# Mish as one ScalarE activation, the key norms' root on VectorE, and a new instruction order in a fused delta-rule and feed-forward kernel

## The chip, the cores and the metric

The kernel runs on one core of a Trainium2 chip. The core has the engines TensorE (PE; PEld is its weight load), VectorE (DVE), ScalarE (ACT), GpSimd (POOL) and SyncE (SP); each runs its own list of instructions in order, and they wait for each other by semaphores. SP and ACT also start DMA transfers here. Matmuls write to PSUM. The metric is the device time of one execution in microseconds (us), the median of several runs.

## The reference, cut to what matters

```python
def _attn_ref(q, k, v, beta):            # B 4, H 8, S 768, D 48
    k_n = k / (np.linalg.norm(k, axis=-1, keepdims=True) + 1e-06)
    for t in range(S):
        y[:, :, t] = q_t @ state
        state = state + beta_t * outer(k_t, v_t - state.T @ k_t)

def _moe_ref(x, w_in, w_out):            # x 3072x384, d_ff 2048
    h = x @ w_in
    sp = np.where(h > 20.0, h, np.log1p(np.exp(np.minimum(h, 20.0))))
    g = h * np.tanh(sp)
    return (g @ w_out).astype(np.float32)
```

The loop is shortened to its algebra (`k_t` stands for the normalised key). `x` is the first part's `y` with the heads put side by side. The function h · tanh(softplus(h)) is called Mish. `w_in` and `w_out` arrive as 64-bit floats; all else is 32-bit.

## The kernel before

**Delta rule in blocks.** The 768 steps are cut into 12 blocks of 64, and 32 batch-head pairs sit in 16 tile columns (`NP`) of two halves. Inside a block the recurrence is solved as a triangular system in two 32-row parts; across blocks a state is carried. `early(g)` prepares the blocks 2g and 2g+1, for g from 0 to 5: it transposes k (`kt`, line 1721), forms the Gram blocks k·k on PE (`pg`, line 1752), masks them into `d` (line 1755) and transposes `d` to `gt` (line 1763) so that one partition holds a whole 32x32 triangle. The diagonal of `gt` is the squared norm of the keys (`ss`); its root `y` is made on ACT by Ln and Exp (lines 1773 and 1774), and DVE forms the factor `nb` with a reciprocal and a few operations on 32 columns. The triangle is scaled by it (line 1790) and solved column by column with a product (`pr`, line 1806) and an addition (line 1808). For g below `FG` = 2 the triangle is *split*: two 16x16 triangles, 14 steps, and a later `merge(n)` for each of the four blocks. A merge has small matmuls `ma` (line 1860) and `mb` (line 1871), an ACT copy `ym`, a DVE addition into `tt` (line 1874) and a transpose; split solves end with transposes to `tu` (line 1816) and `tt` (line 1818). For g of 2 and more the whole triangle is solved in 30 steps; it ends with transposes to `d` (line 1825) and `tn` (line 1829), and POOL copies `d` to `tt` (`place`, line 1841).

**The stages of a block** on PE, in the helper of line 1936, are named by their tiles: `ta` and `tb` (solved triangles applied to the second Gram part), `gq` (queries), `pz` and `py`. Block 2's `ta` is the first thing that needs early 1. The block's output is transposed and split into a high and a low part of x (ACT line 2063, DVE line 2065), both held in a format that PE multiplies exactly enough in three products.

**Feed-forward in units.** Each block gives 256 rows of x. A unit (n, fp), 12 x 8 of them, takes 256 of the 2048 columns: 18 matmuls of 128x256 into `h` (line 2089; two buffers of PSUM), then a chain of eight steps to `g`, then 12 matmuls of 128x384 into `acc` (line 2126). The chain: Exp from `h` on ACT (2103), clamp and +1 on DVE (2104), Square, Ln and Exp on ACT (2105 to 2107), the product with `h` on DVE (2108), a copy to the high part of `g` on ACT (2109) and the subtraction for the low part on DVE (2110). The weights are held negated, which the signs in the chain take into account.

**Weights.** `convert` turns 28 weight parts (12 of `w_in`, 128x512, and 16 of `w_out`, 128x384) from 64-bit patterns to high and low 32-bit parts: a clamp on DVE (line 1665), a Prelu on ACT that adjusts the exponent with its sign (line 1667), a shift and a combination on DVE (1674, 1676), the high part on ACT (1680) and the low part on PE and ACT or on DVE (1697).

**Order.** The order of the instructions of the five engines is fixed by hand: the table `TN` and a long table of numbers ahead of it give each step of each piece (`early0`, `cv5`, `merge2`, `g1.0.3.0>2` and so on) its place, and pieces also wait for labels given by others. Loads go over SP's queue by the helper of line 1621, some over ACT's; k and the second block's q are loaded 32 and then 16 columns wide, after the unused part of the tile was set to zero (line 1710). The `warm` matmuls (line 2152) multiply zeros and have no use in the result.

Of the kernel before, what the change touches and what calls it, by code (L numbers as in the profile page):

```python
# [28 lines left out]
def bcast_in(ap, n):  # L29
# [10 lines left out]
    'loada': [5],  # L40
    'early0': [6, 7, 8, 9, 10, 13, 20, 22, 23, 24, 25, 26, 28, 29, 30, 31, 32, 33, 34, 37, 38, 39, 40, 41, 42, 44, 45, 46, 53, 54, 55, 56, 57, 58, 59, 60, 61],
    'loadv': [11],
    'early0.2>1': [12],
    'early0.1>1': [14],
    'early0.4>1': [15],
    'loadi1': [16],
    'cv0': [69, 17, 87, 96, 113, 114, 134, 166, 164],
    'loads': [18],
    'early0.5>1': [19],
# [19 lines left out]
    'turn_q(0,1,(1,))': [74],
    'turn_q(0,1,(0,))': [75],  # L70
    'cv4': [76, 107, 132, 155, 219, 228, 230, 231, 189],
    'warm30.6': [77],
    'warm29.5': [78],
    'loadi3': [79],
    'unit(1,)': [80],
    'turn_q(0,0,(1,))': [81],
    'cv5': [82, 121, 199, 200, 201, 202, 203, 233, 212],
    'loadp': [83],
# [2319 lines left out]
```

## Time and profile before

| | us |
|---|---|
| median of 3 runs | 689.33 |
| lowest and highest | 685.59, 690.51 |
| the profiled execution | 684.56 |
| its span in the profile | 682.8 |

PE is busy 635.3 us of the span, DVE 489.9, ACT 430.3, POOL 72.1. The profile's page groups instructions by line, engine and tile. A row such as "L2108 DVE SCALAR_TENSOR_TENSOR e<-e,h" gives the tile written and those read, how often, the busy time, the mean of one in ns, the idle time of the engine ahead of them and what ended most of that. A row of waits names the waiting engine, tile and line, then whom it waited for; "issue" stands for time in which no wait is seen. The weight of a wait depends on whether the engine that waits is the one that sets the end of its stretch.

### The profile page before, as it was taken

To read this page: it belongs to the slowest core of one execution; us is meant where nothing else is said; L and a number is where in the kernel's file an instruction comes from. 1 tells how busy PE (TensorE), PEld (TensorE's weight loads), DVE (VectorE), ACT (ScalarE), POOL (GpSimd) and SP (SyncE) were. 2 spreads that over 40 slices of the span, in tenths; PEclk is the share of its full clock that TensorE was granted. 3 is DMA by queue.
4 is the path that set the end of the run, shared out by engine and by line. 5 is a ranking of instruction groups with operands and counts; after the bars stand their busy time and mean duration, and the time that the engine had idled before them with its cause. 6 is when DMAs were issued, how large, how long until landed. Compare 5 with 4: busy or idle time off the path is not lost.

```text
span 682.8 us, 23514 instructions
## 1 busy us (share of the span) xinstructions
PE 635.3 (93%) x10203; PEld 577.8 (85%) x10203; DVE 489.9 (72%) x1042; ACT 430.3 (63%) x802; POOL 72.1 (11%) x119
## 2 busy tenths in 40 slices
...
GB/s 154 164 285 216 213 1 26 1 48 49 5 48 49 64 19 45 62 22 56 36 33 53 45 35 42 48 37 26 42 42 35 22 42 48 25 20 7 1 24 23
DMA packets 161510, 37.79 MB, mean 55 GB/s; under 512 B 154720, under 2 KB 157792, under 8 KB 161408
## 3 DMA queue, kind: packets, MB, share of 16 engines
...
q10 hardware_dynamic: 6464, 0.69, 0.8%
q14 instruction: 22, 0.18, 0.1%
...
## 4 chain that ended last, share of the span: by engine, by line
PE 43%; DVE 35%; ACT 8%; issue 6%; DMA 4%; SPq 4%; ACTq 0%; DVEq 0%
PE h L2089 15%; PE acc L2126 15%; DVE gt L1808 5%; DVE pr L1806 5%; DVE e L2108 4%; DVE g L2110 3%; SPq L1621 3%; DVE xx L1987 3%; PE gq L1936 3%; DVE xx L1923 2%; DMA kt<-in_k_dram 2%; DVE gt L1763 2%; DVE e L2104 2%; DMA xx<-in_q_dram 2%; PE pg L1752 2%
## 5 line engine op out<-in xcount | busy, mean ns | idle before, releaser
L2089 PE MATMUL h<-x,wi 128*128 128x256 f32 x1728 | 232.1, 289 | 17.3 <-DVE e L2108 5.4
L2089 PEld LDWEIGHTS h<-x,wi 128*128 128x128 f32 x1728 | 218.9, 192 | 25.2 <-DVE e L2108 6.7
L2126 PE MATMUL acc<-wo,g 128*128 128x384 f32 x1152 | 225.5, 344 | 4.4 <-DVE g L2110 2.2
L2126 PEld LDWEIGHTS acc<-wo,g 128*128 128x128 f32 x1152 | 199.8, 190 | 10.8 <-DVE g L2110 6.1
L2108 DVE SCALAR_TENSOR_TENSOR e<-e,h 128x512 f32<-128x512 f32 x96 | 65.7, 684 | 76.8 <-ACT e L2107 75.3
L2105 ACT ACTIVATE e<-e 128x512 f32<-128x512 f32 x96 | 60.6, 631 | 54.1 <-DVE e L2104 53.3
L2109 ACT CAST g<-e 128x512 fp32r<-128x512 f32 x96 | 59.3, 618 | 48.5 <-DVE e L2108 47.0
L2110 DVE TENSOR_TENSOR g<-e,g 128x512 fp32r<-128x512 f32 x96 | 68.4, 713 | 28.8 <-ACT g L2109 27.7
L2103 ACT ACTIVATE e<-h 128x512 f32<-128x512 f32 x96 | 57.2, 595 | 42.7 <-PE h L2089 34.2
L2107 ACT ACTIVATE e<-e 128x512 f32<-128x512 f32 x96 | 60.6, 632 | 2.7
L2106 ACT ACTIVATE e<-e 128x512 f32<-128x512 f32 x96 | 60.6, 631 | 2.5
L2104 DVE TENSOR_SCALAR e<-e 128x512 f32<-128x512 f32 x96 | 41.6, 435 | 26.2 <-ACT e L2103 25.8
L1808 DVE TENSOR_TENSOR gt<-gt,pr 128x84 f32<-128x84 f32 (+14 forms) x148 | 51.3, 346 | 3.5
L1806 DVE TENSOR_TENSOR pr<-gt 128x84 f32<-128x84 f32 (+14 forms) x148 | 49.8, 337 | 3.5
L1936 PE MATMUL gq<-xx,kt 48*64 48x112 f32 (+1 forms) x768 | 44.5, 260 | 2.2 <-DVE xx L1923 1.3
L1936 PE MATMUL py<-xx 128*64 128x48 f32 x768 | 43.5, 227 | 2.9 <-ACT xx L2009 2.9
L1936 PEld LDWEIGHTS py<-xx 128*64 128x64 f32 x768 | 39.5, 141 | 7.8 <-ACT xx L2009 3.8
L1936 PEld LDWEIGHTS gq<-xx,kt 48*64 48x64 f32 x768 | 38.3, 136 | 4.4 <-DVE xx L1923 2.2
L1987 DVE TENSOR_TENSOR xx<-gq,amask 64x256 f32<-64x256 f32 x96 | 40.2, 418 | 0.7
L1936 PE MATMUL ps<-xx 128*48 128x48 f32 x704 | 39.0, 211 | 0.4 <-DVE xx L1987 0.2
L1936 PEld LDWEIGHTS pz<-vt,tt 64*64 64x64 f32 x768 | 32.7, 135 | 5.1 <-issue 2.9
L1936 PE MATMUL pz<-vt,tt 64*64 64x48 f32 x768 | 36.6, 231 | 0.0
...
## 6 DMA issues: line engine op xcount, KB each, us to landing
...
```

Of the source, the lines that this page charges most:

```text
L1806: nc.vector.tensor_tensor(out=pv, in0=nj, in1=xj, op=ALU.mult)
L1808: nc.vector.tensor_tensor(out=below, in0=below, in1=pv, op=ALU.add)
L1936: last[:] = [nc.tensor.matmul(*a, start=True, stop=True)]
L1987: nc.vector.tensor_tensor(out=x[r, p4, hh, D:D + C], in0=ps[r, :, d:], in1=bcast_mid(amask[r], 4), op=ALU.mult)
L2089: nc.tensor.matmul(h[:, f2, :], wt["i", f * P // WI * NCH + c][:, i2, f0:f0 + P], x[:, c, :], start=(i == 0), stop=(i == 3 * NCH - 1))
L2105: (0.65, lambda: nc.scalar.activation(e, e, AF.Square)),
L2106: (0.65, lambda: nc.scalar.activation(e, e, AF.Ln, bias=0.5, scale=0.5)),
L2107: (0.7, lambda: nc.scalar.activation(e, e, AF.Exp, scale=-1.0)),
L2108: (0.8, lambda: nc.vector.scalar_tensor_tensor(e, e, -1.0, h, op0=ALU.add, op1=ALU.mult)),
L2109: (0.7, lambda: nc.scalar.copy(out=gg[:, 0], in_=e)),
L2110: (0.8, lambda: eng.tensor_tensor(out=gg[:, 1], in0=e, in1=gg[:, 0], op=ALU.subtract))):
L2126: nc.tensor.matmul(acc[t], gg[:, a, f2, ts_], wt["o", f][:, i2, :], start=(f == 0 and i == 0), stop=(f == NF - 1 and i == 2))
```

## The change

1. The unit's chain has three steps in place of eight: one ACT activation Mish from `h`, with scale -1 for the negated weights, then the copy and the subtraction as before. The very first Mish (block 0) is ordered behind the Prelu of the first 14 weight parts.
2. Weight parts from the 15th on (`KP` = 14; six of 128x512 and eight of 128x384) use an ACT multiplication and one more DVE operation in place of the Prelu.
3. `FG` is 1: early 1 is solved as a whole triangle with 30 steps, merges 2 and 3 do not exist, and POOL's `place` copies blocks 2 and 3.
4. Unsplit Gram blocks are written by the mask operation in the order in which the transpose then reads them contiguously; the transpose to `tn` reads `d`, contiguous too. For g of 1 and more the root of the norms is made on DVE: an integer first guess and two Newton steps, eleven operations on 32 columns in place of ACT's Ln and Exp. For g = 0 Ln and Exp stay.
5. The second half of k (and of block 1's q) is loaded 32 wide, reading into the next row, and the memsets go, but for the last block.
6. The table of places is a new one. ACT has five table loads in place of one; the last stands before the first Mish.

```diff
-    TN = dict(tl=4.0, fg=2, pl=[*range(0, 8)], po=8, ...
+    TN = dict(tl=4.0, fg=1, pl=[*range(0, 8)], po=8, ...
...
-    'merge2': [564, 565, 571, 577],
...
+    def wide_rows(src, hh):
+        flat = src.rearrange("hh t (b h) d -> (hh b h t d)", b=2)
+        rows = flat[32:B * H * S * D - (D - 32)].rearrange("(m d) -> m d", d=D)
+        m0 = hh * (NP * S - C)
+        return rows[m0:m0 + NP * S, 0:32].rearrange("(p t) d -> t p d", t=S)
...
-        nc.scalar.activation(hf, hf, AF.Prelu, scale=2.0 ** -112, alpha=-2.0 ** 32)
+        if k < KP:
+            nc.scalar.activation(hf, hf, AF.Prelu, scale=2.0 ** -112, alpha=-2.0 ** 32)
+            give(f"s{k}")
+        else:
+            nc.scalar.mul(out=hf, in_=hf, mul=2.0 ** -112)
+            yield
+            nc.vector.scalar_tensor_tensor(hf, hf, -2.0 ** 32, hf, op0=ALU.mult, op1=ALU.max)
...
-        for r in (slice(32, 64), slice(96, 128)):
-            (nc.vector if n < 2 else nc.gpsimd).memset(kts[n][r, :, :, D - 32:], 0.0)
...
+                    to = dt[:, t2, pr, :] if split else dg[:, t2, pr, :]
...
+            nc.vector.transpose(gr.rearrange("p a b -> p (a b)")[:, :32 * 32], dt.rearrange("p a b f -> p (a b f)"))
...
-        nc.scalar.activation(y, ss, AF.Ln, scale=0.25)
-        nc.scalar.activation(y, y, AF.Exp, scale=0.5)
+        if g:
+            nc.vector.tensor_scalar(ss, ss, 0.25, None, op0=ALU.mult)
+            yi = y.bitcast(I32)
+            nc.vector.tensor_scalar(yi, ss.bitcast(I32), 1, None, op0=ALU.logical_shift_right)
+            nc.vector.tensor_scalar(yi, yi, 0x1FBD1DF5, None, op0=ALU.add)
+            rn = ap.tile([P, 32], F32, tag="rc", name=f"rn{g}", bufs=1)
+            for _ in range(2):
+                nc.vector.reciprocal(rn, y)
+                nc.vector.scalar_tensor_tensor(rn, ss, 1.0, rn, op0=ALU.mult, op1=ALU.mult)
+                nc.vector.tensor_scalar(y, y, 0.5, None, op0=ALU.mult)
+                nc.vector.scalar_tensor_tensor(y, rn, 0.5, y, op0=ALU.mult, op1=ALU.add)
+        else:
+            nc.scalar.activation(y, ss, AF.Ln, scale=0.25)
+            nc.scalar.activation(y, y, AF.Exp, scale=0.5)
...
-            for d, f in ((0.7, lambda: nc.scalar.activation(e, h, AF.Exp, scale=-1.0)),
-                         (0.55, lambda: nc.vector.tensor_scalar(e, e, EXP20, 1.0, op0=ALU.min, op1=ALU.add)),
-                         (0.65, lambda: nc.scalar.activation(e, e, AF.Square)),
-                         (0.65, lambda: nc.scalar.activation(e, e, AF.Ln, bias=0.5, scale=0.5)),
-                         (0.7, lambda: nc.scalar.activation(e, e, AF.Exp, scale=-1.0)),
-                         (0.8, lambda: nc.vector.scalar_tensor_tensor(e, e, -1.0, h, op0=ALU.add, op1=ALU.mult)),
+            for d, f in ((0.7, lambda: nc.scalar.activation(e, h, AF.Mish, scale=-1.0)),
                          (0.7, lambda: nc.scalar.copy(out=gg[:, 0], in_=e)),
```

What the new order does is seen at three places. In the lists below a name such as `h1_3` is a tile with the block and the unit, the last number only tells tiles apart, and "x3" is a run of three alike. First PE around the start of block 2, before; `tu1` is what the split solve of early 1 leaves:

```order
L2089 MATMUL h1_2_2291<-x0_1_2083,wi5_1417 128x256
L1860 MATMUL ma2_0_2313<-tu1_2286,d1_1615 32x16 x32
L1860 MATMUL ma2_1_2346<-tu1_2286,d1_1615 32x16 x32
L2126 MATMUL acc0_1_2383<-wo0_1245,g1_0_2173 128x384 x3
L2126 MATMUL acc0_1_2383<-wo1_1254,g1_0_2173 128x384 x3
L2126 MATMUL acc1_1_2384<-wo0_1245,g1_0_2173 128x384 x3
L2126 MATMUL acc1_1_2384<-wo1_1254,g1_0_2173 128x384 x3
L1871 MATMUL mb2_0_2397<-tt2_102,ym1_2289 32x16 x32
L1871 MATMUL mb2_1_2435<-tt2_102,ym1_2289 32x16 x32
L1860 MATMUL ma3_0_2474<-tu1_2286,d1_1615 32x16 x32
L2089 MATMUL h1_3_2512<-x0_1_2083,wi3_1393 128x256
```

The same place after, from the end of `h1_3` on:

```order
L1633 MATMUL h1_3_2338<-x0_1_2109,wi5_1386 128x256
L1480 MATMUL ta2_2359<-d1_1490,at2_1491 32x32 x32
L1665 MATMUL acc0_1_2271<-wo2_1226,g1_1_2225 128x384 x3
L1665 MATMUL acc0_1_2271<-wo3_1323,g1_1_2225 128x384 x3
L1665 MATMUL acc1_1_2272<-wo2_1226,g1_1_2225 128x384 x3
L1665 MATMUL acc1_1_2272<-wo3_1323,g1_1_2225 128x384 x3
L1480 MATMUL tb2_2411<-at2_1491,tn1_2336 32x32 x32
L1280 MATMUL pg4_0_2451<-kt4_1245 32x64 x32
L1280 MATMUL pg4_1_2484<-kt4_1245 32x64 x32
L1633 MATMUL h1_4_2535<-x0_1_2109,wi6_1606 128x256
```

Block 2's `ta` stood behind the merge and `h1_3` before; now it reads `d1`, the output of the solve itself, and no merge stands around it.

Second, DVE at the start of the first solve (early 0), before:

```order
L1806 TENSOR_TENSOR pr0_1_347<-gt0_314 128x28
L1808 TENSOR_TENSOR gt0_314<-gt0_314,pr0_1_347 128x2x14
L1806 TENSOR_TENSOR pr0_2_350<-gt0_314 128x52
L1808 TENSOR_TENSOR gt0_314<-gt0_314,pr0_2_350 128x2x13x2
L1806 TENSOR_TENSOR pr0_3_354<-gt0_314 128x72
L1808 TENSOR_TENSOR gt0_314<-gt0_314,pr0_3_354 128x2x12x3
```

And after; `mi` are shifted weights, `ro` raw ones, and `xx` holds the queries:

```order
L1350 TENSOR_TENSOR pr0_1_434<-gt0_321 128x28
L1352 TENSOR_TENSOR gt0_321<-gt0_321,pr0_1_434 128x2x14
L1203 TENSOR_SCALAR mi0_447<-ri0_129 128x512
L1188 TENSOR_SCALAR ro1_331<-ro1_331 128x384
L1350 TENSOR_TENSOR pr0_2_450<-gt0_321 128x52
L1467 STREAM_TRANSPOSE xx0_98<-xx0_98 64x8x64
L1352 TENSOR_TENSOR gt0_321<-gt0_321,pr0_2_450 128x2x13x2
L1467 STREAM_TRANSPOSE xx0_98<-xx0_98 64x8x64
L1467 STREAM_TRANSPOSE xx1_99<-xx1_99 64x8x64
L1350 TENSOR_TENSOR pr0_3_456<-gt0_321 128x72
L1203 TENSOR_SCALAR mi1_461<-ri1_227 128x512
L1352 TENSOR_TENSOR gt0_321<-gt0_321,pr0_3_456 128x2x12x3
```

Transposes of q and conversion steps that stood behind the first solve now stand between its steps.

Third, ACT at the root of the first key norms (`y0`), before:

```order
L1757 COPY at1_219<-pg1_1_261 128x256
L1773 ACTIVATE y0_320<-ss0_318 128x32
L1774 ACTIVATE y0_320<-y0_320 128x32
L2191 COPY betaT_84<-beta_323 128x192
L1621 DMA xx0_98<-in_q_dram 32x8x32 x2
```

And after:

```order
L1286 COPY at1_238<-pg1_1_274 128x256
L1317 ACT_TABLE_LOAD
L1317 ACTIVATE y0_327<-ss0_325 128x32
L1318 ACT_TABLE_LOAD
L1318 ACTIVATE y0_327<-y0_327 128x32
L1191 ACTIVATE ri0_129<-ri0_129 128x512
L1131 DMA xx0_98<-in_q_dram 32x8x32 x2
```

A table load stands before each of the two activations now, and the loads of q are issued behind them and behind a Prelu of the weights. Line numbers in these lists are those of each kernel's own file.

More of the change, by code (lines that the diff above doesn't have):

```diff
@@ L36 @@
     'loadk1': [1],
-    'loadi0': [2],
-    'loadb': [3],
+    'unit(0,)': [2],
+    'loadi0': [3],
     'warm0.5': [4],
[L40 to L49, printed above, removed]
@@ L69 @@
[L69 to L78, printed above, removed]
[89 rows of a table removed]
+    'early0': [5, 8, 10, 12, 16, 18, 22, 27, 32, 34, 38, 40, 43, 48, 49, 50, 53, 54, 55, 58, 59, 60, 61, 62, 63, 64, 65, 66, 67, 68, 69, 70, 71, 72, 73, 74, 75],
+    'loadb': [6],
@@ new lines @@
+    'loadv': [7],
+    'loado2': [9],
+    'early0.2>1': [11],
+    'cv0': [23, 13, 36, 86, 92, 109, 113, 125, 124],
+    'loadi1': [14],
+    'loads': [15],
+    'early0.1>1': [17],
+    'early0.4>1': [19],
+    'turn_beta()': [20],
+    'early0.5>1': [21],
+    'loado1': [24],
+    'loadq': [25],
+    'cv1': [26, 33, 46, 96, 107, 89, 128, 139, 140],
+    'warm8.0': [28],
+    'warm11.5': [29],
+    'scale_v(0,1)': [30],
+    'scale_v(0,0)': [31],
+    'loadk2': [35],
+    'cv4': [37, 51, 154, 157, 216, 223, 227, 228, 190],
@@ new lines @@
+    'turn_q(0,0,(0,))': [39],
+    'turn_q(0,0,(1,))': [41],
+    'turn_q(0,1,(0,))': [42],
+    'loada': [44],
+    'loadi2': [45],
+    'loado3': [47],
+    'loado5': [52],
+    'loadi4': [56],
+    'loadx': [57],
+    'warm30.6': [76],
+    'warm29.5': [77],
+    'loado6': [78],
+    'merge0': [79, 81, 93, 100],
+    'loado4': [80],
+    'loado0': [82],
+    'merge0.0>1': [83],
+    'gq00': [84],
+    'merge0.1>1': [85],
+    'loadi3': [87],
+    'cv5': [88, 144, 197, 201, 203, 209, 210, 222, 215],
@@ L1487 @@
     nc = tc.nc
-    TN = dict(tl=4.0, fg=2, pl=[*range(0, 8)], po=8, pg=(), db=2, sp=21, slow=1.4, ab0=(39.5, 1.45), gqe=(2.,2.), ev=0,
+    TN = dict(tl=4.0, fg=1, pl=[*range(0, 8)], po=8, pg=(), db=2, sp=21, slow=1.4, ab0=(39.5, 1.45), gqe=(2.,2.), ev=0,
               fixed=((1e9,('PE','DVE','Activation','Pool','SP')),),
@@ L1631, in load_src @@
                 w = 32 if ch == 0 else D - 32
+                if ch and n == NS - 1:
+                    nc.gpsimd.memset(dst[64 * (1 - hh) + 32:64 * (1 - hh) + 64, :, :, D - 32:], 0.0)
                 for tb in range(2):
@@ L1634, in load_src @@
                     r0 = 64 * (1 - hh) + 32 * ch
-                    load(dst[r0:r0 + 32, :, tb, :w], src[hh, t0:t0 + 32, :, 32 * ch:32 * ch + w])
+                    if ch and n < NS - 1:
+                        load(dst[r0:r0 + 32, :, tb, :], wide_rows(src, hh)[t0 + C * hh:t0 + C * hh + 32])
+                    else:
+                        load(dst[r0:r0 + 32, :, tb, :w], src[hh, t0:t0 + 32, :, 32 * ch:32 * ch + w])
         turns[0] = False
@@ L1754, in out @@
                 def out(t2=t2, ps=ps, at=at, pr=slice(8 * h8, 8 * h8 + 8)):
-                    nc.vector.tensor_tensor(out=dt[:, t2, pr, :], in0=ps[:, :, 32:],
+                    to = dt[:, t2, pr, :] if split else dg[:, t2, pr, :]
+                    nc.vector.tensor_tensor(out=to, in0=ps[:, :, 32:],
                                             in1=bcast_mid(lmask, 8), op=ALU.mult)
@@ L1762, in early @@
         gt = gr[:, :32]
-        nc.vector.transpose(gt, dt.rearrange("p a b f -> p f (a b)"))
+        if split:
+            nc.vector.transpose(gt, dt.rearrange("p a b f -> p f (a b)"))
+        else:
+            nc.vector.transpose(gr.rearrange("p a b -> p (a b)")[:, :32 * 32], dt.rearrange("p a b f -> p (a b f)"))
         gf = gt.rearrange("p a b -> p (a b)")
@@ L1772, in early @@
         y = ap.tile([P, 32], F32, tag="y", name=f"y{g}", bufs=1)
[L1773 to L1774 removed]
+        if g:
[9 more added lines that the diff above has]
+                nc.vector.scalar_tensor_tensor(y, rn, 0.5, y, op0=ALU.mult, op1=ALU.add)
+        else:
+            nc.scalar.activation(y, ss, AF.Ln, scale=0.25)
+            nc.scalar.activation(y, y, AF.Exp, scale=0.5)
         yield ("b",)
@@ L1777, in early @@
         nc.vector.reciprocal(rc, y)
-        nc.vector.scalar_tensor_tensor(ss, ss, 0.25, rc, op0=ALU.mult, op1=ALU.mult)
+        nc.vector.scalar_tensor_tensor(ss, ss, 1.0 if g else 0.25, rc, op0=ALU.mult, op1=ALU.mult)
         nc.vector.scalar_tensor_tensor(ss, ss, 1e-6, y, op0=ALU.add, op1=ALU.add)
@@ L1826, in early @@
             give(f"T{g}")
-            yield (f"B{2 * g - 1}",)
+            yield (f"B{2 * g - 1}",) if g else ()
             tn = tns[g] = ap.tile([P, 2, NP, 32], F32, tag="tn", name=f"tn{g}", bufs=1)
-            nc.vector.transpose(tn.rearrange("p a b j -> p j (a b)"), gt.rearrange("p i j -> p j i"))
+            nc.vector.transpose(tn.rearrange("p a b j -> p (a b j)"), dt.rearrange("p a b i -> p (a b i)"))
             give(f"N{g}")
-            yield [f"z{2 * g - 2}{h}" for h in range(2)]
+            yield [f"z{2 * g - 2}{h}" for h in range(2 if g else 0)]
             place(g, 0)
-            yield [f"z{2 * g - 1}{h}" for h in range(2)]
+            yield [f"z{2 * g - 1}{h}" for h in range(2 if g else 0)]
             place(g, 1)
@@ L2098, in g1 @@
                 gg = mp.tile([P, 2, 2, UT], F32R, tag="g", name=f"g{n}_{fp}", bufs=3)
-            eng = nc.gpsimd if n in TN['pg'] else nc.vector
             step = 0
             t, slow = (2.8, TN['slow']) if n < 1 else (2.4, 1.0)
-            for d, f in ((0.7, lambda: nc.scalar.activation(e, h, AF.Exp, scale=-1.0)),
-                         (0.55, lambda: nc.vector.tensor_scalar(e, e, EXP20, 1.0, op0=ALU.min, op1=ALU.add)),
-                         (0.65, lambda: nc.scalar.activation(e, e, AF.Square)),
-                         (0.65, lambda: nc.scalar.activation(e, e, AF.Ln, bias=0.5, scale=0.5)),
-                         (0.7, lambda: nc.scalar.activation(e, e, AF.Exp, scale=-1.0)),
-                         (0.8, lambda: nc.vector.scalar_tensor_tensor(e, e, -1.0, h, op0=ALU.add, op1=ALU.mult)),
+            for d, f in ((0.7, lambda: nc.scalar.activation(e, h, AF.Mish, scale=-1.0)),
                          (0.7, lambda: nc.scalar.copy(out=gg[:, 0], in_=e)),
-                         (0.8, lambda: eng.tensor_tensor(out=gg[:, 1], in0=e, in1=gg[:, 0], op=ALU.subtract))):
+                         (0.8, lambda: nc.vector.tensor_tensor(out=gg[:, 1], in0=e, in1=gg[:, 0], op=ALU.subtract))):
                 step += 1
-                defer(t, f, need=(f"m{n}.{fp}.{step - 1}",) if step > 1 else (), label=f"m{n}.{fp}.{step}")
+                first = [f"s{k}" for k in range(KP)] if n == fp == 0 else ("m0.0.1",) if n == 0 else ()
+                defer(t, f, need=(f"m{n}.{fp}.{step - 1}",) if step > 1 else first, label=f"m{n}.{fp}.{step}")
                 t += d * slow
@@ L2214, in loads @@
             q1[0] = ap.tile([P, NP, 2, 32], F32, tag="kt", name="q1", bufs=4)
-            for r in (slice(32, 64), slice(96, 128)):
-                nc.gpsimd.memset(q1[0][r, :, :, D - 32:], 0.0)
             load_src(q1[0], qq, 1)
```

30 lines of the change are left out of this document (6 added, 24 removed), and 2259 rows, old and new, of the table TT.

## The prediction

> **What bounds the kernel now.** I read the page's head first, then the busy time of each engine in four stretches that I cut at the places where the new order changes something, then the waits inside these stretches, and last the groups of instructions for prices. Head of the page:
>
> ```profile
> span 682.8 us, 23514 instructions
> ```
>
> The stretches (columns: us, busy time of PE, PEld, DVE, ACT, POOL with counts, granted clock, DMA share, GB/s). I call them A, B, C and D. A ends when the low part of block 0's x is made; B ends when DVE has solved the triangles of blocks 2 and 3 (early 1); C ends where `h1_5` starts on PE; D is the rest but for 3.9 us.
>
> ```profile
> 0.00:66.50 66.50, 58.25 (x1162) 34.46 (x1162) 43.35 (x103) 22.13 (x46) 15.35 (x35) 0.87 0.89 200
> 66.50:160.20 93.70, 78.05 (x1245) 68.38 (x1246) 82.20 (x185) 59.90 (x118) 7.38 (x11) 0.91 0.30 68
> 160.20:193.60 33.40, 29.57 (x1032) 27.65 (x1031) 20.11 (x39) 18.77 (x39) 6.65 (x11) 0.90 0.07 13
> 193.60:678.90 485.30, 469.44 (x6768) 447.31 (x6766) 344.23 (x719) 329.44 (x600) 42.72 (x62) 1.00 0.21 36
> ```
>
> So the bound differs. In D it is PE: 469.4 of 485.3 us busy, only 15.9 us idle. In B it is DVE, 82.2 of 93.7, and PE idles 15.6 us. A few waits show who is late. First PE's waits: three rows of D, then one of B, then one of C (total us, times, longest):
>
> ```profile
> PE h L2089 <- DVE e L2108: 4.6, 6, 1.9
> PE acc L2126 <- DVE g L2110: 2.2, 4, 0.7
> PE acc L2126 <- ACT g L2109: 1.1, 2, 0.6
> ...
> PE ma L1860 <- DVE tu L1816: 2.5, 1, 2.5
> ...
> PE mb L1871 <- issue: 3.1, 2, 1.6
> ```
>
> In D, 7.9 us of PE's idle time end with a step of the unit chain (product, subtract, copy). In B, PE waits 2.5 us for `tu`, the end of the solve: DVE sets the start of block 2. And DVE's own idle time in B:
>
> ```profile
> DVE e L2104 <- ACT e L2103: 4.5, 2, 3.8
> DVE e L2108 <- ACT e L2107: 1.4, 3, 0.8
> DVE g L2110 <- ACT g L2109: 0.9, 2, 0.7
> ```
>
> 6.8 of its 11.5 idle us stand behind ACT inside that same chain.
>
> **The unit chain.** Groups by line (busy us, mean ns of one, then idle before):
>
> ```profile
> L2103 ACT ACTIVATE e<-h 128x512 f32<-128x512 f32 x96 | 57.2, 595 | 42.7 <-PE h L2089 34.2
> L2104 DVE TENSOR_SCALAR e<-e 128x512 f32<-128x512 f32 x96 | 41.6, 435 | 26.2 <-ACT e L2103 25.8
> L2107 ACT ACTIVATE e<-e 128x512 f32<-128x512 f32 x96 | 60.6, 632 | 2.7
> L2108 DVE SCALAR_TENSOR_TENSOR e<-e,h 128x512 f32<-128x512 f32 x96 | 65.7, 684 | 76.8 <-ACT e L2107 75.3
> ```
>
> Per unit this takes 0.435 + 0.684 = 1.12 us from DVE and three ACT passes of about 0.63 (Square, Ln, Exp) from ACT. Mish on ACT does not occur in the trace; its nearest row is the Exp that reads the same `h`, 595 ns, and the other functions on the same tile take 632, so I take 0.6 us; how high it could be is a rival below. `h` is now released after that one pass, where the product at the chain's sixth step held it.
>
> In D the three waits above lose their cause, 7.9 us. The rest of the 15.9 ends with DMA, x and xx, where DVE is only rid of some load; I take 1.1 us of it. D: **-9**, between 0 (the waits only change their name) and -15.9 (no idle left). If the chain's cover is gone, DVE's subtract is late next, as it shares DVE with the next blocks' solves.
>
> **B: DVE gets more to do.** The solve of early 1 goes from the split form (14 steps) to the whole triangle (30). The trace has both forms: early 1 in B, and the four unsplit ones later. Lines 1806 and 1808, DVE busy in B and in the rest:
>
> ```profile
> 66.50:160.20 93.70, 3.96 (x14) 0.91 0.30 68
> 190.00:683.00 493.00, 41.95 (x120) 1.00 0.22 36
> ...
> 66.50:160.20 93.70, 3.38 (x14) 0.91 0.30 68
> 190.00:683.00 493.00, 43.82 (x120) 1.00 0.22 36
> ```
>
> Split: 7.34 us. Unsplit: (41.95 + 43.82) / 4 = 21.44. That is +14.10. The other prices, by form, and two single instructions of B's end from the timeline:
>
> ```profile
> L1763 DVE STREAM_TRANSPOSE gt<-d 128x1024 f32<-128x1024 f32 x6 | 12.1, 2010 | 0.1
> L1721 DVE STREAM_TRANSPOSE kt<-kt 128x1024 f32<-128x1024 f32 x12 | 14.9, 1240 | 3.0 <-DMA kt<-in_k_dram 2.9
> L1825 DVE STREAM_TRANSPOSE d<-gt 128x1024 f32<-128x1024 f32 x4 | 8.1, 2028 | 0.1
> L1790 DVE TENSOR_TENSOR gt<-gt,nb 128x1024 f32<-128x1024 f32 x4 | 4.9, 1225 | 0.1
> L1790 DVE TENSOR_TENSOR gt<-gt,nb 128x512 f32<-128x512 f32 x2 | 1.4, 692 | 0.1
> L1676 DVE SCALAR_TENSOR_TENSOR mi<-ri,mi 128x512 int32<-128x512 int32 x9 | 6.1, 690 | 0.2
> L1676 DVE SCALAR_TENSOR_TENSOR mo<-ro,mo 128x384 int32<-128x384 int32 x12 | 6.5, 550 | 0.1
> L1780 DVE RECIPROCAL rc<-ss 128x32 f32<-128x32 f32 x6 | 2.1, 354 | 0.2
> L1779 DVE SCALAR_TENSOR_TENSOR ss<-ss,y 128x32 f32<-128x32 f32 x6 | 1.2, 193 | 0.2
> ...
> 157.34 1.06 DVE L1816 STREAM_TRANSPOSE tu<-gt 128x512 f32<-128x512 f32 x1
> 158.30 1.90 DVE L1818 STREAM_TRANSPOSE tt<-gt 128x1024 f32<-128x1024 f32 x1
> ```
>
> Step by step: the two scalings of the block (lines 1790 and 1810) on 1024 columns in place of 512, 2 x (1.225 - 0.692) = +1.07. One output transpose of 2.03 in place of 1.06 + 1.90 = -0.93. The Gram block is now read contiguously; its transpose of 2.01 becomes like that of k, 1.24, which is already contiguous: -0.77 (0 if only the writing strided costs). The root on DVE: 2 reciprocals and 9 small operations, 2 x 0.354 + 9 x 0.193 = +2.44. Fourteen weight parts get a DVE operation after a multiplication on ACT; like line 1676 it reads two tiles, 6 x 0.69 + 8 x 0.55 = +8.54; ACT's multiplication takes the place of a Prelu of equal shape, 0. Sum +24.45. Taken away: of the units of block 0 in B about 10 clamps and 9 products, 10 x 0.435 + 9 x 0.684 = -10.51. Net **+13.9**: DVE busy 96.1. Its idle time falls from 11.5 to 4.7, since the 6.8 behind the chain go; B lasts 100.8 in place of 93.7, **+7.1** (ends: +2.4 with no idle time, +13.9 with all of it kept).
>
> **A: the first solve.** Rows on which it rests (timeline of DVE and PE, and two groups):
>
> ```profile
> 65.50 1.02 DVE L2065 TENSOR_TENSOR x<-xt,x 128x384 fp32r<-128x384 f32 x2 [9.42 <-ACT x L2063]
> ...
> 45.90 3.59 PE L2152 MATMUL warm<-zero 128*128 128x512 bf16 x8
> ...
> L1923 DVE STREAM_TRANSPOSE xx<-xx 64x512 f32<-64x512 f32 x44 | 31.1, 706 | 6.6 <-DMA xx<-in_q_dram 5.4
> ...
> L2200 ACT ACT_TABLE_LOAD x1 | 1.3, 1283 | 7.1 <-DMA kt<-in_k_dram 7.1
> ```
>
> The one table load hid ahead of the first data. Now there are five, and one stands between the Ln and the Exp of the first key norms, on the way to the solve: +1.28; the others lie at places where ACT idles (22.1 of 66.5 busy), 0, and after the first Mish there are none. Three transposes of `xx` and a few conversion steps go in between the solve's steps; they stood behind the solve but before the same next use, so I expose one, +0.71 (0 to 3 x 0.71). The eight warm-up matmuls between `ta0` and `tb0` go, -3.59. A: **-1.6**, ends -3.6 and +3.4. The Trainium skill, page "ScalarE: Activation LUTs", section "What ACT_TABLE_LOAD costs", charges a switch with a drain of about 1.38 us beside the load of 1283 ns. The trace agrees on the load and shows no drain; by the page, A would be -0.2 and the time below 1.4 us longer, an estimate.
>
> Loads of k and of block 1's q with 32 columns in place of 16 for their second half: 3 tiles x 4 x 32 KB = 0.39 MB more in A, 2 us at the 200 GB/s of its row. The number of rows fetched stays, so I take 0, the 2 us stay in the range. Fewer memsets on POOL and DVE: 0, both wait for DMA there.
>
> **C: merges.** Merge 2 and 3 end. What stands of them between block 2's `ta` and `h1_5` (two rows of PE's timeline; then lines 1871 and 1860 in that stretch):
>
> ```profile
> 167.69 1.20 PE L1936 MATMUL ta<-tt,at 32*32 32x32 f32 x64
> 193.62 0.64 PE L2089 MATMUL h<-x,wi 128*128 128x256 f32 x4
> ...
> 167.60:193.60 26.00, 1.84 (x128) 1.47 (x128) 0.93 0.07 13
> ...
> 167.60:193.60 26.00, 0.76 (x64) 0.67 (x64) 0.93 0.07 13
> ```
>
> Their matmuls, 1.84 + 0.76 = 2.6 us, and the 3.1 us that `mb` waited. The granted clock is 0.90 in C and 1.00 in D; without the small matmuls and waits I take half of a tenth of some 20 us, 1.0. C: **-6.7**, ends -2.6 and -7.7. POOL gets eight copies for blocks 2 and 3; it is busy 6.65 of 33.4 us, and the copies stand beside PE's acc matmuls: 0, at most +3.3 if half of POOL's work there became exposed.
>
> **Sum.** Before, `ta` of block 2 came 7.5 us after the triangle (160.2 to 167.69) because merge 2 lay between; now it reads the triangle itself. It comes at 160.2 - 1.6 + 7.1 + 0.2 = 165.9, so A and B together bring -1.8. With C and D: -1.8 - 6.7 - 9 = -17.5. Span 665.3; the profiled execution, 684.56 (1.76 around the span), becomes 667.1. That execution lies 0.7% under the median of the three runs, 689.33 (685.59 to 690.51); on the median's scale it is 671.7. I forecast the middle, **669.5**.
>
> **Rivals.**
> 1. DVE late, no change. B keeps all 11.5 us of idle time (4.7 of it has other causes, and the added wait of block 0's first Mish for 14 Prelus may put something in the chain's place), and A ends at +3.4. `ta` of block 2 then comes 3.4 + 13.9 - 7.3 = 10.0 later; with C and D -5.7: 678.9 here, 683.6 on the median's scale. For it: DVE is the busiest engine in B and gets 14 us. Against: 6.8 of the idle us have their cause removed. Chance 0.13.
> 2. D gains nothing: the chain's waits fall to x, xx or the subtract, as D's PE is at 97% already. -8.5: 676.1 to 680.7. Chance 0.08.
> 3. All idle time goes: A -3.6, B +2.4 (`ta` at -8.5), C -7.7, D -15.9, together -32: 652.5 to 657. For it: DVE loses a unit of 1.12 us 96 times. Against: waits on DMA are in the rest. Chance 0.15.
> 4. Slower: Mish is much dearer than Exp. D has some 80 units; ACT is busy 329.4 - 80 x 3 x 0.63 = 178 us there with Mish at 0.6. PE needs 476, so each Mish may take (476 - 178) / 80 = 3.7 us more, 4.3 in all, before ACT sets D. At 6 us D would last 610, the whole about 800. Against: 595 to 632 ns for each function of the rows. Chance 0.04.
>
> **How the numbers follow.** The forecast has 0.60, its own range 662 to 677. The range 656 to 682 leaves out rival 4, half of rival 1 and half of rival 3, 0.18 in all, and the 2 us of DMA lie in it. About 1% is what a measurement here can tell from no change: 682.4 to 696.2. Faster by more: 0.59 of the forecast, 0.15, 0.07 of rival 2, 0.05 of rival 1, together 0.86; within: 0.10; slower: 0.04.
>
> **What would show it.** In the profile after: Mish near 600 ns and no table load behind the first (else rival 4); the low part of block 0's x at about 64 (65.5 before); the transpose to `d` of early 1 ending near 166 with DVE busy 94 to 98 us between (later than 172 is rival 1); no `ma`, `mb` behind block 2's `ta`, and `h1_5` some 19 us after it; PE idle time behind that near 7 us, without h waiting for `e` (15 or more is rival 2). The forecast is wrong if DVE's added operations cost more than the rows of like shape, or if the conversions, now with one more step through DVE, hold up the weights that block 0's units need.

## The result, and the profile after

| | before | after |
|---|---|---|
| median of 4 runs, us | 688.40 (685.59 to 690.51) | 672.44 (671.19 to 673.84) |
| span of the profiled execution, us | 682.8 | 669.4 |

The ratio is 0.9766, 95% interval 0.9741 to 0.9791: faster by 2.3%. The forecast was 669.5 with a range of 656 to 682. The total hides large errors in its parts, which the same four stretches show. Their ends are found in the profile after by the same events: the low part of block 0's x is made, block 2's `ta` starts, `h1_5` starts, 3.9 us before the end (columns as in the prediction's table of stretches; here the second stretch runs to `ta`):

```profile
0.00:69.24 69.24, 55.07 (x1156) 35.05 (x1161) 42.04 (x99) 26.05 (x49) 14.52 (x31) 0.85 0.87 200
69.24:176.40 107.16, 81.55 (x1170) 73.40 (x1158) 95.50 (x221) 45.26 (x90) 3.21 (x5) 0.86 0.28 64
176.40:197.43 21.03, 19.81 (x619) 18.33 (x619) 13.95 (x33) 10.15 (x21) 6.38 (x9) 0.92 0.07 13
197.43:665.50 468.07, 464.32 (x6767) 448.84 (x6766) 268.36 (x590) 182.20 (x346) 36.76 (x55) 1.00 0.23 38
```

With the same ends, the kernel before has 66.5, 101.2, 25.9 and 485.3 us. So:

| stretch | forecast | measured |
|---|---|---|
| A, to the low part of x | -1.6 | +2.7 |
| B, on to `ta` of block 2 | -0.2 | +6.0 |
| C, on to `h1_5` | -6.7 | -4.9 |
| D, the rest | -9 | -17.2 |
| sum | -17.5 | -13.4 |

The prices of single operations, from the groups by form (busy us, mean ns):

```profile
L1646 ACT ACTIVATE e<-h 128x512 f32<-128x512 f32 x96 | 57.2, 598 | 148.9 <-PE h L1633 143.5 <-DVE g L1648 5.0
...
L1295 DVE STREAM_TRANSPOSE gt<-d 128x1024 f32<-128x1024 f32 x5 | 6.2, 1244 | 0.1
L1196 DVE SCALAR_TENSOR_TENSOR ro<-ro 128x384 f32<-128x384 f32 x8 | 4.3, 554 | 0.0
L1196 DVE SCALAR_TENSOR_TENSOR ri<-ri 128x512 f32<-128x512 f32 x6 | 4.1, 687 | 0.7 <-ACT ri L1194 0.7
```

Mish costs what Exp costs, 598 ns on 128x512. The contiguous transpose and the added operations cost what the rows of like shape said. What the forecast missed are the waits. In B, PE's and DVE's:

```profile
PE h L1633 <- DVE x L1609: 5.7, 1, 5.7
PE acc L1665 <- DVE wo L1226: 5.6, 2, 3.8
PE h L1633 <- ACT e L1646: 4.6, 1, 4.6
PE acc L1665 <- DVE g L1648: 3.4, 1, 3.4
...
DVE mi L1203 <- PE loo L1217: 3.3, 1, 3.3
DVE g L1648 <- ACT g L1647: 1.5, 3, 0.8
DVE tt L1418 <- PE mb L1415: 1.4, 2, 1.1
```

PE now waits in B for everything that DVE makes: x of block 1, converted weights, g. DVE is busy 95.5 of 107.2 us there; its idle time is no longer that of the unit chain but first of all that of the conversions, whose step on PE (`loo`) stands late. The 4.6 us behind `e` are a wait for the very first Mish: it starts at 91.7 us, right behind the last of the 14 Prelus and a table load. In D the long waits for the chain are gone: the 15.9 us of idle time before are 3.8 now.

### The profile page after: what moved, and what is told of

It reads as the page before. It is cut to its first block, busy times and chain, and to the rows that moved or that the text cites. A ratio compares the mean times of both kernels' runs of the same rounds, so it can differ in the third digit from the quotient of the medians.

```text
span 669.4 us, 22061 instructions
## 1 busy us (share of the span) xinstructions
PE 620.8 (93%) x9687; PEld 575.6 (86%) x9691; DVE 419.9 (63%) x941; ACT 263.7 (39%) x504; POOL 60.9 (9%) x100
## 4 chain that ended last, share of the span: by engine, by line
PE 71%; DVE 17%; DMA 3%; issue 3%; SPq 3%; ACT 2%; ACTq 0%; DVEq 0%
PE acc L1665 26%; PE h L1633 25%; PE gq L1480 5%; PE py L1480 3%; DVE gt L1352 3%; SPq L1131 3%; DVE pr L1350 3%; PE ps L1480 2%; DMA kt<-in_k_dram 2%; PE pg L1280 2%; PE pz L1480 2%; PE ta L1480 2%; PE tb L1480 1%; DMA xx<-in_q_dram 1%; DVE xx L1531 1%
## 5 line engine op out<-in xcount | busy, mean ns | idle before, releaser
L1633 PE MATMUL h<-x,wi 128*128 128x256 f32 x1728 | 226.7, 286 | 12.1 <-DVE x L1609 5.9
L1665 PEld LDWEIGHTS acc<-wo,g 128*128 128x128 f32 x1152 | 203.3, 192 | 14.9 <-DVE wo L1226 6.1
L1350 DVE TENSOR_TENSOR pr<-gt 128x58 f32<-128x58 f32 (+9 forms) x164 | 57.8, 353 | 4.7
L1352 DVE TENSOR_TENSOR gt<-gt,pr 128x58 f32<-128x58 f32 (+9 forms) x164 | 56.4, 344 | 4.9
L1467 DVE STREAM_TRANSPOSE xx<-xx 64x512 f32<-64x512 f32 x44 | 31.1, 706 | 27.4 <-DMA xx<-in_q_dram 26.5
L1480 PE MATMUL py<-xx 128*64 128x48 f32 x768 | 41.8, 225 | 0.6 <-ACT xx L1553 0.6
L1553 ACT COPY xx<-pz 64x384 f32<-64x384 f32 x48 | 22.8, 474 | 44.9 <-PE gq L1480 25.9
L1385 POOL COPY tt<-d 32x512 f32<-32x512 f32 x40 | 26.0, 650 | 123.1 <-DVE d L1369 64.1
L1480 PEld LDWEIGHTS ps<-xx 128*48 128x48 f32 x704 | 32.0, 125 | 1.1 <-DVE xx L1531 1.1
L1456 POOL TENSOR_TENSOR vt<-vt,ne 128x384 f32<-128x384 f32 x24 | 21.0, 886 | 115.5 <-DMA vt<-in_v_dram 115.0
```

The source lines that it names most:

```text
L1350: nc.vector.tensor_tensor(out=pv, in0=nj, in1=xj, op=ALU.mult)
L1352: nc.vector.tensor_tensor(out=below, in0=below, in1=pv, op=ALU.add)
L1385: nc.gpsimd.tensor_copy(out=tt2[r, t2, :, c0:c0 + 32], in_=dts[g][r, t2])
L1467: nc.vector.transpose(x, x)
L1480: last[:] = [nc.tensor.matmul(*a, start=True, stop=True)]
L1553: (nc.vector.tensor_copy if hh and n < TN['ev'] else nc.scalar.copy)(out=x[r, :, hh, 0:D], in_=pz[r])
```

## The experiments

Each ratio is to executions of the kernel before that were taken together with it; their medians lie between 687.7 and 688.4 us in all four sets. "After" without a label is the changed kernel, 0.9766 (0.9741 to 0.9791), 671.2 to 673.8 us.

**The chain alone, in the old order.** The question is what of the gain belongs to the short chain, and what to the new order and the rest.

```diff
 # kernel before
-            for d, f in ((0.7, lambda: nc.scalar.activation(e, h, AF.Exp, scale=-1.0)),
...
+            for d, f in ((0.7, lambda: nc.scalar.activation(e, h, AF.Mish, scale=-1.0)),
+                         (0.55, lambda: None), ...
+        prelu = k in (0, 1, 2, 3, 4, 5, 6, 7, 8, 10, 11, 15)
...
+        if not prelu:
+            nc.vector.scalar_tensor_tensor(hf, hf, -2.0 ** 32, hf, op0=ALU.mult, op1=ALU.max)
```

> The kernel before, with its own order of places, two split solves and the narrow loads; only the unit chain is Mish, copy, subtract, and what ACT needs for it (16 weight parts by multiplication and a DVE operation, the root of the norms on DVE for g of 1 and more). It has two table loads. Theory 1, the shorter chain is what the stretch behind h1_5 gained: that stretch, 485.3 us before and 468.1 after, falls to 467 to 472 here too, and the time is 668 to 674 (ratio 0.970 to 0.979). Theory 2, the new order is the source: that stretch stays above 480 and the time is 682 to 688 (0.991 to 1.0).

Measured: 0.9861 (0.9782 to 0.9940), 679.10 us. The next kernel differs only in where the copy and the subtraction stand.

```diff
 # k1_chain_alone: the places of steps 7 and 8 of each unit
-    'g1.n.fp.0>7': [place of the old copy],
-    'g1.n.fp.0>8': [place of the old subtraction],
+    'g1.n.fp.0>7': [place of the old clamp],
+    'g1.n.fp.0>8': [place of the old second Exp],
```

> As k1_chain_alone (old order, only the chain and what it needs), but the copy and the subtraction of each unit stand at the places of the old clamp and the old second Exp, right behind the Mish, not at their own old, late places. If the remaining gain of the last stretch (468.1 us after, 474.4 in k1_chain_alone) comes from where the short chain stands in the order: 467 to 471 here, and the time 671 to 676. If it comes from something else of the change: 473 to 476, and the time as k1_chain_alone, 677 to 681.

Measured: 0.9874 (0.9791 to 0.9958), 676.73 us. The last stretch of both (first k1_chain_alone, then k9_chain_tight):

```profile
199.16:673.60 474.44, 465.58 (x6767) 448.72 (x6766) 272.35 (x597) 176.85 (x345) 42.81 (x62) 1.00 0.22 36
```

```profile
195.66:669.10 473.44, 466.11 (x6767) 450.04 (x6766) 273.07 (x595) 182.94 (x345) 41.04 (x62) 0.99 0.22 36
```

485.3 becomes 474.4 and 473.4: the chain alone gives 11 to 12 of the 17.2 us of D, between the two theories. The 1 us by which k9_chain_tight is shorter is no more than D varies: in ten profiles whose units in D are those of the changed kernel it is 467.6 to 470.0 us. The other 5 to 6 us come with the new order or one of the smaller edits; which one was not tried. The waits of the weight loads in D say that they are not the chain's: from k9_chain_tight to the changed kernel those for `x` fall from 2.6 to 0.4 us and the time in which no wait is seen from 8.9 to 4.5. Outside D neither kernel gains: DVE's busy time in B is 90 us for 87 before, since the added weight operations outweigh what the chain gave up, B is 104 to 107 us for 101, and the merges keep C at 26 to 27 us.

**How much the chain's length matters in D.** The opposite edit, on the changed kernel:

```diff
+            def mish():
+                nc.scalar.activation(e, h, AF.Mish, scale=-1.0)
+                if n > 1:
+                    nc.scalar.activation(e, h, AF.Mish, scale=-1.0)
```

> The changed kernel with the Mish of every unit from block 2 on done twice in a row (the second writes the same values). ACT is busy 182 of 468 us in the last stretch. If PE bounds it and ACT has room as the prediction's rival 4 worked it out (3.7 us a unit), 80 more Mishes of 0.6 us cost under 1 us. If the chain's length still sets PE's waits, the stretch grows by 3 us or more.

Measured: 0.9863 (0.9829 to 0.9897), 678.25 us, against 0.9766 without it. Its last stretch, and whom the weight loads of `acc` wait for there:

```profile
198.54:672.50 473.96, 466.64 (x6767) 449.08 (x6766) 267.08 (x590) 228.82 (x426) 36.48 (x55) 1.00 0.22 38
```

```profile
PEld acc L1670 <- DVE g L1653: 1.7, 4, 0.4
...
PEld acc L1670 <- ACT g L1652: 1.2, 3, 0.5
```

ACT is busy 229 of 474 us, half of the stretch, and still 0.6 us more between `h` and `g` cost 5.9 us over 80 units. The first guess (ACT has room, so it is free) fell. What fits is that D feels the time from a unit's `h` to the release of its buffer and to its `g`, since there are only two buffers of `h` and each `acc` stands a unit or two behind. The trace shows it in part: the waits of the weight loads that name a step of the chain grow from 1.3 to 4.4 us, and the rest of the 5.9 lies in waits for `x` and in time in which no wait is seen. That the second Mish also holds up ACT's other work was not separated from it.

**DVE and the start of block 2.**

```diff
-            nc.vector.tensor_tensor(out=pv, in0=nj, in1=xj, op=ALU.mult)
+            if g != 1 or j < 15:
+                nc.vector.tensor_tensor(out=pv, in0=nj, in1=xj, op=ALU.mult)
...
-            nc.vector.tensor_tensor(out=below, in0=below, in1=pv, op=ALU.add)
+            if g != 1 or j < 15:
+                nc.vector.tensor_tensor(out=below, in0=below, in1=pv, op=ALU.add)
```

> The changed kernel, but the last 16 of the 30 steps of early 1's solve are left out (32 DVE operations, 10.6 us busy in the profile after), so blocks 2 and 3 use a half-solved triangle. Theory 1, DVE's work sets the start of block 2 and this start sets the rest: ta of block 2 comes at about 165 in place of 176.4 and the time falls by 8 to 11 us, to 661 to 665. Theory 2, PE has other work to fill and is the bound over the whole: ta comes earlier, but the time falls by less than 3 us (669 to 673).

Measured: 0.9673 (0.9603 to 0.9742), 663.53 us, 8.9 us under the changed kernel. B and C of this run:

```profile
71.27:169.84 98.57, 79.22 (x1175) 72.07 (x1164) 87.43 (x191) 45.24 (x90) 5.33 (x8) 0.90 0.28 67
169.84:189.12 19.28, 18.34 (x620) 17.04 (x619) 11.58 (x30) 10.16 (x21) 3.88 (x7) 1.00 0.14 24
```

DVE is busy 8.1 us less in B and B is 8.6 us shorter; with A 2.0 us longer, C 1.7 shorter and D the same 468.2, the span falls by 8.2 us: DVE's work in B is paid in full. `ta` comes at 169.8 and not at 165, because A of this run is 2 us longer and because DVE's busy time fell by 8.1 us and not by 10.6. Was the whole triangle a bad trade, then?

```diff
-    TN = dict(tl=4.0, fg=1, ...
+    TN = dict(tl=4.0, fg=2, ...
+    'merge2': [551, 551.2, 552.4, 552.6],
+    'merge3': [561, 561.1, 574.5, 574.6],
```

> The changed kernel with early 1 split again (14 steps) and merges 2 and 3 back at places around block 2's ta; all else as changed. Theory 1, DVE's work sets the start of block 2: DVE has some 15 us less ahead of the triangle, the triangle comes 11 to 14 us earlier, merge 2 takes 4 to 6 us of it back, so ta of block 2 comes at 166 to 170 (176.4 in the profile after); the stretch from it to h1_5 is 23 to 26 us (21.0), and the time falls by 2 to 6 us. Theory 2, the whole triangle was worth it, since the merges' small matmuls and waits cost more than 30 steps that run beside other work: the time stays within 1.5 us or rises.

Measured: 0.9877 (0.9781 to 0.9973), 676.94 us, slower than the whole triangle: its runs begin at 675.4 us, where those of k7_pool_sub below, of the same set and with the whole triangle, end at 674.5. B and C, and the transpose that ends the split solve:

```profile
68.34:172.86 104.52, 84.43 (x1455) 75.75 (x1455) 85.84 (x195) 45.50 (x92) 6.22 (x11) 0.87 0.29 66
172.86:204.01 31.15, 27.90 (x875) 26.12 (x875) 13.65 (x36) 10.61 (x23) 1.66 (x4) 0.73 0.06 11
...
L1362 DVE STREAM_TRANSPOSE tu<-gt x1: 1060/1060/1060, 161.8 to 161.8; 128x512 f32<-128x512 f32 x1
```

The triangle comes 12.6 us earlier (161.8; the changed kernel's last transpose starts at 174.4), but `ta` only 3.5, since merge 2 and the units among it take the rest, and C is 10.1 us longer at a granted clock of 0.73. So the time rose, as theory 2 has it, for these places of the merges; others were not tried. But the small matmuls and waits that it names are only part of it. The clock is granted in full or at half here (18 matmuls of `h` take 2.40 or 4.11 us), so a mean of 0.73 over 31.15 us takes 8.4 us of PE's work, and 0.92 over 21.03 us takes 1.7. By this estimate 6.7 of the 10.1 us go with the clock; whether the merges bring it about is not shown. In the kernel before most of merge 3 stands in C too, at 0.93.

The same load was taken from DVE in two more ways. First, block 0's eight subtractions on GpSimd:

```diff
-                         (0.8, lambda: nc.vector.tensor_tensor(out=gg[:, 1], ...
+                         (0.8, lambda: (nc.vector if n else nc.gpsimd).tensor_tensor(out=gg[:, 1], ...
```

> The changed kernel with the subtraction for the low part of g of block 0's eight units on GpSimd in place of VectorE. If DVE's work sets the start of block 2, 8 x 0.7 = 5.6 us less of it bring ta of block 2 forward by 3 to 6 us and the time down by 2 to 6 us. If GpSimd's slower subtraction or its queue makes acc wait instead, or the two engines slow each other, ta moves by less than 2 us and the time stays within 2 us or rises.

Measured: 0.9804 (0.9739 to 0.9870), 672.75 us: nothing. DVE's busy time in B stayed at 95.8 us with seven instructions fewer. Why, two timelines show, GpSimd's and DVE's at the same moment of that run, and DVE's same instruction in the changed kernel:

```profile
122.44 1.30 POOL L1648 TENSOR_TENSOR g<-e,g 128x512 fp32r<-128x512 f32 x1 [4.30 <-ACT g L1647]
...
122.72 1.07 DVE L1303 TENSOR_SCALAR ss<-gt 128x32 f32<-128x32 f32 x1
```

```profile
123.00 0.19 DVE L1303 TENSOR_SCALAR ss<-gt 128x32 f32<-128x32 f32 x1
```

This DVE instruction meets GpSimd's subtraction and ends only when that ends: 1.07 us in place of 0.19. Not every instruction is held up so; a reciprocal and operations that read PSUM kept their time beside a subtraction. But in sum DVE lost about what the moved subtractions, 0.69 us each, had freed.

Second, the 14 weight parts back on Prelu, with a table load at each change between Prelu and Mish:

```diff
-            nc.scalar.mul(out=hf, in_=hf, mul=2.0 ** -112)
-            yield
-            nc.vector.scalar_tensor_tensor(hf, hf, -2.0 ** 32, hf, op0=ALU.mult, op1=ALU.max)
+            nc.scalar.activation(hf, hf, AF.Prelu, scale=2.0 ** -112, alpha=-2.0 ** 32)
+            yield
```

> The changed kernel with the Prelu on ACT for all 28 weight parts, so DVE is rid of the 14 operations that came with the multiplication (8.4 us busy in the profile after), and ACT gets six more table loads between Prelus and Mishes (7.7 us; ACT is busy 45 of the 107 us of that stretch). If DVE's work sets the start of block 2: its ta 5 to 8 us earlier than 176.4, the time 4 to 8 us less. If the table loads, or block 0's units behind them, take its place: less than 2 us.

Measured: 0.9730 (0.9696 to 0.9763), 669.34 us, 3.1 us under the changed kernel, with six loads more. All its runs (666.3 to 670.8) lie below all of the changed kernel's, though the intervals of the two ratios overlap. B, and DVE's largest wait in it:

```profile
69.71:173.46 103.75, 79.62 (x1174) 71.73 (x1162) 88.50 (x208) 52.87 (x96) 3.21 (x5) 0.88 0.29 66
```

```profile
DVE g L1647 <- ACT g L1646: 4.8, 4, 2.5
```

DVE has 7.0 us less to do and B is 3.4 us shorter; most of the rest went into DVE's wait for `g`, 4.8 us in place of 1.5. The longest of these, 2.5 us, ends behind a table load at 117.7 us, the Mish and the copy. That is between the two expectations.

**A and the late first solve.** Three edits of the places in the changed kernel:

```diff
 # k3_preload
-    'loada': [44],
+    'loada': [4.5],
 # k4_q_late
-    'turn_q(0,0,(0,))': [39],  'turn_q(0,0,(1,))': [41],  'turn_q(0,1,(0,))': [42],
+    'turn_q(0,0,(0,))': [75.2],  'turn_q(0,0,(1,))': [75.3],  'turn_q(0,1,(0,))': [75.4],
 # k10_solve_whole: k3_preload, and early 0's solve in one piece
-    'early0': [..., 32, 34, 38, 40, 43, 48, 49, ..., 75],
+    'early0': [..., 32, 34, 34.6, 34.61, 34.62, 34.63, 34.64, ..., 34.86],
```

> The changed kernel with the set of Ln and Exp loaded ahead of the first ACT instruction, so that two table loads remain in place of five. If the loads ahead of Ln and Exp delay the first solve (2.6 us of ACT between 16.02 and 18.93, and q's loads are issued behind them), the low part of block 0's x comes 1.5 to 3 us earlier than 68.2 and the time falls by 1 to 3 us. If they are hidden: under 0.7 us either way.

Measured: 0.9789 (0.9733 to 0.9846), 672.32 us; x's low part done at 70.3. No gain from three table loads fewer: the solve began 0.6 us earlier and lasted as long, 15.4 us for 15.2.

> The changed kernel with the three transposes of q taken out of the steps of early 0's solve and put right behind it, as before the change. If the wait for q's DMA inside the solve (2.56 us) and the three transposes (2.1 us) are what made the first stretch 2.7 us longer, the end of the solve comes 4.5 us earlier (tu at 32.4 in place of 36.9), the low part of block 0's x 2 to 4 us earlier, and the time falls by 1.5 to 4 us. If that part is bound by something else (gq, the second merge matmuls, the conversions), x moves by less than 1 us.

Measured: 0.9788 (0.9728 to 0.9848), 672.92 us; `tu` at 35.8, x at 68.8. The steps of the solve end 1.1 us earlier only: in that run it began 1.8 us later, and DVE waited 1.7 us for a Prelu whose result stands among the solve's steps. Neither says much, because A itself varies by 3 us from run to run: in five profiles with the same first part (after, k2, k6, k7, k11) it is 69.2, 71.3, 68.3, 69.8 and 69.5.

> The changed kernel with early 0's solve in one piece on DVE again (nothing of q or of the conversions between its steps) and with the Ln and Exp set loaded ahead. If the late end of that solve (tu at 36.9 us, 30.0 before the change) is what sets the first stretch, tu comes at 29 to 32, the low part of block 0's x ends at 64 to 67 (69.2 in the profile after; 68.3 to 71.3 in four runs with the same first part), and the time falls by 2 to 4 us. If the moved work only comes back behind the solve, under 1 us.

Measured: 0.9747 (0.9712 to 0.9783), 670.25 us. Its A and B, and DVE's longest wait in B:

```profile
0.00:65.31 65.31, 55.86 (x1150) 33.91 (x1156) 41.35 (x99) 22.42 (x46) 13.99 (x31) 0.87 0.89 212
65.31:175.31 110.00, 84.10 (x1175) 75.54 (x1164) 95.54 (x221) 45.30 (x90) 3.21 (x5) 0.83 0.27 62
```

```profile
DVE mi L1203 <- PE loo L1217: 5.1, 1, 5.1
```

A is 65.3, below all five, and 67.4 in k13_both below, which has the same first part. The solve lasts 10.2 us in these two and 13.0 to 15.2 in the five, while from the first merge's `ma` to x it takes 31.2 and 30.3 us here and 31.1 after: the late solve did set A's end. But in this run DVE's work in B is the same 95.5 us and its idle time grew by 2.8, most of it (1.8) in the wait for `loo`; so `ta` comes 1.1 us earlier, not 3.9. What A gains, B mostly takes back here, and the runs (669.1 to 672.7) overlap those of the changed kernel.

Another idea for A was the granted clock, which is half for 20.5 us from the idle time ahead of `ma` on:

```diff
-    warm=[(0.5,13),(8.0,2),(11.5,66), ...
+    warm=[(0.5,13),(8.0,2),(11.5,94),(33.0,8), ...
+    'warm33.0': [82.5],
```

> The changed kernel with 28 more warm-up matmuls while the first solve runs and 8 between the first merge's ma and gq, where the kernel before had them. In the profile after, PE idles 6.3 us ahead of ma and the clock is granted at half for 20.5 us from then on, before the change for 10.2. If that clock is what makes the first stretch long: half-clock time falls to 12 us or less and the low part of block 0's x ends at 65.5 to 67.5 in place of 69.2; time -1.5 to -3.5 us. If DVE and the waits for data set that stretch: it stays between 68.2 and 70.5 and the time within 1 us.

Measured: 0.9855 (0.9786 to 0.9924), 675.90 us, slower; x at 72.8. `tu` started at 36.7 as before, but PE was still in its warm-ups until 41, so the edit delayed what it was to help. It does say something on the clock: the time at half fell to some 10 us, as expected, and from `ma` to x it still took 31.7 us, 1.9 of them the eight warm-ups, for 31.1 after. So the clock is not what sets that part, or by no more than a microsecond or two.

**Both.** k10_solve_whole and k12_prelu_all in one kernel:

> k10_solve_whole and k12_prelu_all together. If the two act on two stretches that follow each other, their gains add: 660 to 667 us. If what the first stretch gives is lost in the wait for DVE in the second, or the other way round, no better than the better of the two.

Measured: 0.9699 (0.9651 to 0.9746), 666.16 us. It is the lowest median of all that solve every triangle in full, 3.0% under the kernel before; the interval touches that of the changed kernel and overlaps that of k12_prelu_all. The median is within what adding gains would give, but the runs spread from 662.8 to 672.4, and the profiled one, of 670.4 us, has A at 67.4, B at 107.5 and `ta` at 174.9, later than in k12_prelu_all alone (173.5). That the two gains add is not shown.

## Why the prediction was right, and where its steps failed

The two large mechanisms were those named: the short chain helps D, and DVE's added work costs B. Of the sizes, D's and B's were wrong, and in A even the sign. That the time came within 3 us is in part luck: the errors, +4.3 in A, +6.2 in B, +1.8 in C and -8.2 in D, cancel to +4.1.

*The unit chain.* Its price was right, 598 ns for 600. "In D the three waits above lose their cause, 7.9 us" was right too, but as the size of D's gain it was too small: D fell by 17.2, beyond the end of 15.9 that the prediction gave as "no idle left". The step that failed is to take PE's idle time for all that PE loses. PE's busy time in D also fell, by 5.1 us for the same matmuls (469.4 to 464.3), though the mean of one stayed (341 ns for `acc`, 284 and 283 for `h`). The records of matmuls overlap: the 1021 of `acc`, 341 ns each, are busy only 197.6 us before and 195.0 after. So a pause counts as idle only from the end of the last record on, and a short one not at all. The weight loads show more of it. Their rows in D, before and then after:

```profile
L2089 PEld LDWEIGHTS h<-x,wi 128*128 128x128 f32 x1494 | 185.2, 188 | 12.2 <-DVE e L2108 5.8 <-DVE x L2065 2.5 <-issue 1.6
L2126 PEld LDWEIGHTS acc<-wo,g 128*128 128x128 f32 x1020 | 175.0, 188 | 8.8 <-DVE g L2110 5.7 <-ACT g L2109 1.4
...
L1633 PEld LDWEIGHTS h<-x,wi 128*128 128x128 f32 x1494 | 185.5, 188 | 2.0 <-DVE x L1609 0.4
L1665 PEld LDWEIGHTS acc<-wo,g 128*128 128x128 f32 x1020 | 175.6, 188 | 3.9 <-ACT g L1647 0.6 <-DVE g L1648 0.3
```

For `acc` the weights are `g`, and the weight load waits 7.1 us for it where PE's own rows have 3.3. With the 5.8 of `h` that makes 12.9 us behind the chain, and 0.9 after. The chain alone confirms the size: 2.2 us are left of it in k1_chain_alone and none in k9_chain_tight, and D fell by 10.9 and 11.9. In all, PEld is idle 38.0 us of D before and 19.2 after at nearly the same busy time (447.3 and 448.8). Rival 2, that the waits only change their name, is out. Rival 4's limit, 3.7 us more for each Mish before ACT sets D, was not the one that counts: with 0.6 us more k11_two_mish is far from it and already costs 5.8 us in all.

*B.* DVE's work was summed rightly: 96.1 forecast, 95.5 measured. The step that failed is "its idle time falls from 11.5 to 4.7, since the 6.8 behind the chain go". They went, and others came: DVE idles 11.7 us in B after, first of all for the conversions' step on PE. With A this is rival 1 almost whole: it had A at +3.4 and block 2's `ta` 10.0 us later with all of DVE's idle time kept, and measured are +2.7 and 8.7. Its sign, a solve of early 1 that ends later than 172, came too (its transpose ends at 176.3). Only D, which gained twice the forecast, kept the time at the forecast and away from rival 1's 683.6. That DVE's time there is paid one for one, k2_short_solve shows.

*A.* "They stood behind the solve but before the same next use, so I expose one, +0.71" failed. The same next use was not what mattered: the first merge on PE starts with `tu`, ahead of it, and `tu` came 6.9 us later. 1.7 of that is the later start of the solve, of which the load between Ln and Exp is 1.3, as forecast:

```profile
16.02 1.28 ACT L1317 ACT_TABLE_LOAD   x1
17.40 0.23 ACT L1317 ACTIVATE y<-ss 128x32 f32<-128x32 f32 x1
17.65 1.28 ACT L1318 ACT_TABLE_LOAD   x1
18.94 0.23 ACT L1318 ACTIVATE y<-y 128x32 f32<-128x32 f32 x1
...
27.66 0.70 DVE L1467 STREAM_TRANSPOSE xx<-xx 64x512 f32<-64x512 f32 x1 [2.56 <-DMA xx<-in_q_dram]
36.94 1.07 DVE L1360 STREAM_TRANSPOSE tu<-gt 128x512 f32<-128x512 f32 x1
```

The other 5.2 us lie between the solve's steps, 2.56 of them a wait for q's DMA, which the order put in front of the steps that needed no q. `ma` started 5.6 us later and `tb` 3.4, so 2.2 of the freed warm-ups' 3.6 us showed by then. k10_solve_whole confirms the place. A load of tables costs 1.29 us here, from its start at 17.65 to that of the next activation at 18.94; the 1.38 of the load ahead of it hold a wait for `ss`. The Trainium skill, page "ScalarE: Activation LUTs", section "What ACT_TABLE_LOAD costs", adds a drain of about 1.38 us to the load of 1.28. These rows show no such drain.

*C.* Forecast at 19.2 us, measured 21.0 in the profile after, where the clock is granted at 0.92. In the four runs that had it at 1.00 there (k2, k3, k7, k11) it is 19.3 to 19.6, and in five others at 0.92 (k4, k8, k10, k12, k13) 20.8 to 21.6: the sum was near and the clock's share was the part that varies.
